# One more buffer slot, the first dV from a direct product, dO in pages and early flat rows in a decode-attention gradient kernel

## The chip, the cores and the metric

The kernel runs on one core of a Trainium2 chip. The metric is the device time of one execution in microseconds (us); executions of one kernel are repeated and their median is quoted with the range. The profile shows the work of five engines, each with its own order of instructions (TensorE, VectorE, ScalarE, GpSimd; SyncE issues transfers alone), and of 16 DMA engines, which move the data. The granted clock is the share of TensorE's full clock that it was given at a time.

## The reference

A forward pass of two residual blocks for one decode step of 4 sequences, and the gradients of everything. What costs time are the caches: K and V of 4 x 32 heads x 4096 x 128 bf16, 134 MB each.

```
def A_ref(x, k_cache, v_cache, wq, wo):
    q = (x @ wq) as B,H,1,Dh
    p = softmax(q k^T * Dh**-0.5)
    return (p v) as B,1,H*Dh  @ wo
def B_ref(x, w1, w3, w2):
    return (silu(x w1) * (x w3)) w2
h  = x + A_ref(layernorm(x), k_cache, v_cache, wq, wo)
h2 = h + B_ref(layernorm(h), w1, w3, w2)
_out, vjp = jax.vjp(f, x, k_cache, v_cache, wq, wo, w1, w3, w2)
return (h2, *vjp(grad_out))
```

K and V are read once forward, V once more backward, and dK and dV, as large as K and V, are written: five passes over 134 MB of the 708 MB that the kernel moves.

## The kernel before

The forward pass streams K and V through page slots of 4160 bf16 per partition (one head of 1.05 MB each). (A write of a page is called dV or dK with the number of its head, so dV 0 is the first.) Then comes a serial middle: output projection, layer norm, the gated block and its gradient, up to dh, the gradient at the first residual. Only with dh can dO = wo dh, and with that the first dV, be made. The backward loop then reads V, writes dV and dK of each head, and does the weight gradients as side work in between. Oflat is the attention output O laid out flat, one row per sequence, as the gradient of wo needs it; V^T is the transposed V page of a head.

```python
NSLOT = 22
free = deque(range(NSLOT))           # slots are handed out first in, first out

def dO_heads(h0, h1, ps, tag, ps_, tag_):        # heads h0..h1 of dO
    for h in range(h0, h1):
        for jj in range(DC):
            nc.tensor.matmul(dOT_ps[:, h*B:(h+1)*B], lhsT=wo_page(h)[:, h % 8, jj, :], rhs=dhT[:, jj, :], ...)
    ... # columns to bf16, rows by a transposition, and the sums c_rep

# end of the middle
        V_T(0, psT)                              # 32 transposes of V of head 0
        ... # dhT
        dO_heads(0, 8, psC, "cols", psA, "rT")

# side work, ahead of the wo gradient
            pt = psg.tile([P, Dh], BF16, tag="gps", name="pt_O")
            nc.tensor.transpose(pt[:], OT_bf[:], ident_b[:])
            nc.scalar.copy(out=O_sb[:], in_=pt[:])
            oflat = Slot("oflat")
            for b in range(B):
                nc.gpsimd.dma_start(out=oflat.b(HD)[b:b + 1, :], in_=O_sb[b::B, :])
            for _ in range(6):
                yield
...
        def rest_of_dO():
            while wo_units:
                woT_unit(psT, wo_units.popleft(), "s")
                yield
            dO_heads(8, H, psg, "gps", psg, "gps")     # pages 1 to 3 in one block
...
        def grad_V(s):
            gv = Slot("gv")
            outer(gv.heads(), P2s.pop(s), reps["rdo", s // REP][:, s % REP, :])   # VectorE, 128x4096
            nc.gpsimd.dma_start(out=rows_of(out_3[b, h]), in_=gv.heads())
            gv.give()
...
        S0 = 8
        P_pairs(0)
        front(0)              # rows of dO and q in all partitions, V^T, dP of head 0
        grad_V(0)
        for s in range(NH):
            prefetch()        # loads of V
            if s + 1 < NH:
                front(s + 1)
                grad_V(s + 1)
            grad_K(s)
            if s < S0: step("o")
            else:      step("s", ...)
```

## Time and profile before

| | before |
|---|---|
| median of the first 3 runs | 1735.95 us (1733.18 to 1737.97) |
| profiled span | 1737.6 us |
| bytes moved | 707.85 MB |
| TensorE, VectorE, ScalarE, GpSimd busy | 76, 72, 55, 28% |

The prediction shows the lines that say what bounds it: the DMA row is at 9 nearly everywhere. What it did not show are the edges of the second hole and the tail. These are lines of the view by windows; the last two columns are the mean busy share of the 16 DMA engines and GB/s.

```profile
1506.00:1508.00 2.00, 0.00 (x0) 0.00 (x0) 2.00 (x2) 0.00 (x0) 0.00 (x0) 0.50 0.46 191
...
1512.00:1514.00 2.00, 0.00 (x0) 0.00 (x0) 0.58 (x1) 0.00 (x0) 0.78 (x2) 0.50 0.47 195
...
1722.00:1724.00 2.00, 0.00 (x0) 0.00 (x0) 0.00 (x0) 0.00 (x0) 0.00 (x0) 0.50 0.93 389
1724.00:1726.00 2.00, 0.00 (x0) 0.00 (x0) 0.00 (x0) 0.00 (x0) 0.00 (x0) 0.50 0.76 320
1726.00:1728.00 2.00, 0.00 (x0) 0.00 (x0) 0.00 (x0) 0.00 (x0) 0.00 (x0) 0.50 0.43 180
1728.00:1730.00 2.00, 0.00 (x0) 0.00 (x0) 0.00 (x0) 0.00 (x0) 0.00 (x0) 0.50 0.26 111
1730.00:1732.00 2.00, 0.00 (x0) 0.00 (x0) 0.00 (x0) 0.00 (x0) 0.00 (x0) 0.50 0.09 37
```

In the hole the share of these windows never falls under 0.28 (1508 to 1510, shown in the prediction): some of the 16 engines are working all the time. And at the end the share does not drop from 1 to 0 but fades over some 10 us: the engines do not end together.

### The profile page before, as it was taken

Reading aid. Unit: us, or ns where it says so; the run is one execution under the profiler, and the core shown is the slowest. Engines: PE = TensorE matmul, PEld = TensorE weight load, DVE = VectorE, ACT = ScalarE, POOL = GpSimd, SP = SyncE. Lnnn points to the kernel's source line nnn. Section 1 sums busy time; section 2 is a strip of 40 time slices with the busy share of each in tenths; the row PEclk is TensorE's granted clock in tenths of the full one; section 3 lists DMA queues with packets and bytes.
Section 4 is the critical chain, followed back from the end, with each engine's and each line's share of the span. In section 5 each row is a group of like instructions: output and inputs, shape, how many; then the busy total and the mean of one; then the engine's idle time right before and its main releaser. Section 6 shows DMA issues by size and latency. Waiting matters only on the chain.

```text
span 1737.6 us, 43932 instructions
## 1 busy us (share of the span) xinstructions
PE 1324.3 (76%) x18996; PEld 1114.6 (64%) x18996; DVE 1252.8 (72%) x1385; ACT 955.0 (55%) x1464; POOL 493.6 (28%) x815
## 2 busy tenths in 40 slices
PE   5889888888888888877887887577677677488662
PEld 4777776777666667767776776566555555366561
DVE  5899899889999996676666676565654656566574
ACT  3455445444444454655565555476667666377552
POOL 2333333333333331232223122132222212233231
PEclk8999999999999999655555555577557555555655
DMA  9999999999999999899999999999999999999997
GB/s 397 410 418 418 419 418 419 419 412 418 418 415 397 418 407 396 321 388 416 414 413 415 417 412 416 422 423 423 419 412 418 414 414 414 373 400 408 410 419 315
DMA packets 107042, 707.85 MB, mean 407 GB/s; under 512 B 11024, under 2 KB 18840, under 8 KB 23904
## 3 DMA queue, kind: packets, MB, share of 16 engines
q1 hardware_dynamic: 66880, 422.60, 59.3%
q0 software_dynamic: 39968, 282.44, 39.9%
q8 instruction: 149, 2.44, 0.5%
q14 instruction: 45, 0.37, 0.1%
HBM read 422.58 MB, written 282.34 MB: 406 GB/s over the span
## 4 chain that ended last, share of the span: by engine, by line
DMA 43%; DVE 5%; ACT 4%; PE 3%; issue 2%; POOL 1%; POOLq 0%; DVEq 0%; ACTq 0%
DMA out_dram<-gk 20%; DMA out_dram<-gv 18%; ACT VT L759 3%; DMA V<-in_A_v_cache_dram 3%; DVE gk L1096 2%; DVE gv L1096 2%; PE pt_tps L758 2%; DMA out_dram<-gw 2%; DMA oflat<-O_sb 1%; PE gps L891 1%; POOL P L1080 0%; PE dP_ps L1090 0%; ACT reps L1071 0%; PE rep_ps L1068 0%; ACT gwo L885 0%
## 5 line engine op out<-in xcount | busy, mean ns | idle before, releaser
L759 ACT COPY VT<-pt_tps 128x1024 bf16<-128x1024 bf16 x512 | 492.5, 1015 | 278.1 <-PE pt_tps L758 157.6
L758 PE MATMUL pt_tps<-ident_b,V 128*128 128x128 bf16 x4096 | 451.5, 292 | 130.3 <-ACT VT L759 121.6
L758 PEld LDWEIGHTS <-V 128*128 128x128 bf16 x4096 | 400.2, 137 | 193.2 <-issue 177.3
L1096 DVE TENSOR_TENSOR gv<-P,reps 128x4096 bf16<-128x4096 bf16 x128 | 293.0, 2290 | 225.0 <-DMA out_dram<-gk 77.8
L1096 DVE TENSOR_TENSOR gk<-dS,reps 128x4096 bf16<-128x4096 bf16 x128 | 293.7, 2295 | 113.8 <-DMA out_dram<-gv 87.2
L421 DVE TENSOR_TENSOR PK<-Kn,PK 128x4096 bf16<-128x4096 bf16 x128 | 302.9, 2367 | 35.3 <-POOL PK L417 35.3
L436 PE MATMUL M_ps<-PK,Vn 128*128 128x130 bf16 x4096 | 287.8, 223 | 46.8 <-DMA Vn<-in_A_v_cache_dram 46.3
L436 PEld LDWEIGHTS <-Vn 128*128 128x128 bf16 x4096 | 254.7, 100 | 67.1 <-DMA Vn<-in_A_v_cache_dram 59.6
L328 DVE STREAM_TRANSPOSE KT<-Kn 128x512 f32<-128x512 f32 (+1 forms) x321 | 250.9, 798 | 0.5 <-issue 0.5
L323 ACT COPY KT<-pt_tps 128x1024 bf16<-128x1024 bf16 x128 | 129.4, 1012 | 191.3 <-PE pt_tps L322 160.1
L1090 PE MATMUL dP_ps<-dOT_bf,VT 128*128 128x1 bf16 x4096 | 152.1, 166 | 73.4 <-ACT VT L759 63.5
L1090 PEld LDWEIGHTS <-VT 128*128 128x128 bf16 x4096 | 141.1, 104 | 86.3 <-ACT VT L759 75.1
L1121 POOL DMA_DIRECT2D out_dram<-gk x128 | 68.1, 532 | 369.2 <-DVE gk L1096 275.5
L417 POOL COPY PK<-P_all 128x64 bf16<-128x64 bf16 x128 | 32.3, 252 | 437.1 <-ACT P_all L411 424.8
L336 POOL COPY zq<-qT_bf 128x2 bf16<-128x2 bf16 x128 | 152.1, 1189 | 0.0
L1107 POOL DMA_DIRECT2D out_dram<-gv x128 | 68.5, 535 | 287.4 <-DVE dSt L1114 200.3
L1080 POOL COPY P<-P_all 128x64 bf16<-128x64 bf16 x128 | 119.2, 932 | 0.0
L411 ACT COPY P_all<-pt_P 32x64 bf16<-32x64 bf16 x256 | 51.9, 203 | 57.5 <-PE pt_P L407 55.3
L322 PE MATMUL pt_tps<-ident_b,Kn 128*128 128x128 bf16 x1024 | 80.9, 224 | 0.7 <-DVE qrep L282 0.7
L322 PEld LDWEIGHTS <-Kn 128*128 128x128 bf16 x1024 | 62.3, 100 | 26.5 <-issue 26.5
L446 PE MATMUL kP_ps<-PK,onesw 128*32 128x512 bf16 x1024 | 79.3, 386 | 0.0
L400 ACT ACTIVATE Pn<-E,rl 128x1024 bf16<-128x1024 f32 x64 | 73.7, 1151 | 2.8 <-DVE rl L397 2.8
(227 smaller groups left out, 1298.5 us busy)
## 6 DMA issues: line engine op xcount, KB each, us to landing
Kn<-in_A_k_cache_dram SPq DMA_DIRECT2D x128, 1024.0 KB, 14.8
Vn<-in_A_v_cache_dram SPq DMA_DIRECT2D x128, 1024.0 KB, 15.2
V<-in_A_v_cache_dram SPq DMA_DIRECT2D x128, 1024.0 KB, 11.0
out_dram<-gv POOLq DMA_DIRECT2D x128, 1024.0 KB, 24.5
out_dram<-gk POOLq DMA_DIRECT2D x128, 1024.0 KB, 24.0
wq<-in_A_wq_dram SPq DMA_DIRECT2D x8, 1024.0 KB, 13.9
out_dram<-gw POOLq DMA_DIRECT2D x6, 896.0 KB, 27.1
wo<-in_A_wo_dram SPq DMA_DIRECT2D x4, 1024.0 KB, 12.0
```

The costliest lines, as they stand in the source:

```text
L322: nc.tensor.transpose(pt[:, i, :], Kn[:, c * GW + i, :], ident_b[:])
L323: nc.scalar.copy(out=KT[:, c * GW:(c + 1) * GW, :], in_=pt[:])
L328: nc.vector.transpose(out=KT[:, c * w_:(c + n) * w_], in_=Kn[:, c * w_:(c + n) * w_])
L336: nc.gpsimd.tensor_copy(out=zq[gi % 2][hl][:, 32:132:67], in_=qT_bf[:, s:s + 1].to_broadcast([P, 2]))
L421: nc.vector.tensor_tensor(out=PK[:, :, 0:Dh].rearrange("p j (r t) -> p j r t", t=2), in0=Ks[s].heads().rearrange("p j (r t) -> p j r t", t=2),
L436: nc.tensor.matmul(hold["M"][:], lhsT=Vn[:, j, :], rhs=PK[:, j, :], start=(j == 0), stop=(j == SJ - 1))
L446: nc.tensor.matmul(hold["kP"][32 * q:32 * (q + 1), :, :], lhsT=ones_window(w), rhs=PK[:, j0:j0 + 4, 0:Dh], start=(w == 0 and c == 0), stop ...
L758: nc.tensor.transpose(pt[:, i, :], Vn[:, g * GW + i, :], ident_b[:])
L759: nc.scalar.copy(out=VT[:, g * GW:(g + 1) * GW, :], in_=pt[:])
L1080: nc.gpsimd.tensor_copy(out=P2s[s][:], in_=P_all[:, s, :, None].to_broadcast([P, SJ, 2]))
L1090: nc.tensor.matmul(dP_ps[:, j:j + 1], lhsT=VT[:, j, :], rhs=dOT_bf[:, s:s + 1], start=True, stop=True)
L1096: nc.vector.tensor_tensor(out=dst.rearrange("p j (r t) -> p j r t", t=2), in0=col2[:, :, None, :].to_broadcast([P, SJ, Dh // 2, 2]), in1=r ...
```

## The change

The intent: take row tiles out of the permanent memory (xhat, gr, hhat, q rows and single buffers in the forward pass) so that a 23rd slot fits; make the first dV depend on less; spread pages 1 to 3 of dO over the loop; and keep the four row copies of oflat off GpSimd's queue. The core of the diff:

```diff
-NSLOT = 22
+NSLOT = 23
@@ forward: single buffers @@
-        W = fw.tile([P, G, 4, 32], BF16, name="W", tag="W")
+        W = fw.tile([P, G, 4, 32], BF16, name="W", tag="W", bufs=1)
@@ middle, before the gate products: the q rows are made here now @@
+        pq = psA.tile([P, Dh], BF16, tag="rT", name="pq_rows")
+        nc.tensor.transpose(pq[:], qT_bf[:], ident_b[:])
+        nc.scalar.copy(out=qrows_bf[:], in_=pq[:])
         woT(2, "vs")
@@ end of the middle @@
-        V_T(0, psT)
+        V_T(0, psT, range(2))
 ... # dhT
-        dO_heads(0, 8, psC, "cols", psA, "rT")
+        ps = psA.tile([P, B, Dh], FP32, tag="rT", name="rep_ps")
+        for b in range(B):
+            for jj in range(DC):
+                nc.tensor.matmul(ps[:, b, :], lhsT=dhT[:, jj, b:b + 1].to_broadcast([P, P]), rhs=wo_page(0)[:, 0, jj, :],
+                                 start=(jj == 0), stop=(jj == DC - 1))
+        nc.scalar.copy(out=rep_bufs["rdo"][0], in_=ps[:])
+        ... # dO_columns(0, 8, ...)
+        V_T(0, psT, range(2, SJ // GW))
@@ side work: oflat before the w1/w3 gradients, on ScalarE's queue, no yields @@
+            oflat = Slot("oflat")
+            for b in range(B):
+                nc.scalar.dma_start(out=oflat.b(HD)[b:b + 1, :], in_=O_sb[b::B, :])
@@ rest of dO @@
-            dO_heads(8, H, psg, "gps", psg, "gps")
+            for pg in range(1, H // 8):
+                ... # wo transposes of this page
+                dO_columns(8 * pg, 8 * pg + 8, psg, "gps")
+                dO_rows(8 * pg, 8 * pg + 8, psg, "gps")
+                mid_w["wo"][pg].give()
                 yield
@@ start of the loop @@
-        S0 = 8
+        S0 = 9
         P_pairs(0)
+        P_pairs(1)
+        grad_V(0)
+        dO_rows(0, 8, psg, "gps")
         front(0)
-        grad_V(0)
+        step("o")
```

## The prediction

> **What bounds the kernel now.** I read the page's header rows first, then the table of busy time by stretches of 2 us, then the timeline around the stretches where the transfers thin out.
>
> ```profile
> span 1737.6 us, 43932 instructions
> PE 1324.3 (76%) x18996; PEld 1114.6 (64%) x18996; DVE 1252.8 (72%) x1385; ACT 955.0 (55%) x1464; POOL 493.6 (28%) x815
> ...
> DMA  9999999999999999899999999999999999999997
> GB/s 397 410 418 418 419 418 419 419 412 418 418 415 397 418 407 396 321 388 416 414 413 415 417 412 416 422 423 423 419 412 418 414 414 414 373 400 408 410 419 315
> DMA packets 107042, 707.85 MB, mean 407 GB/s; under 512 B 11024, under 2 KB 18840, under 8 KB 23904
> ```
>
> No engine is at 80%; the 16 DMA engines are busy nearly everywhere. At 418 GB/s, the rate of the quiet slices, 707.85 MB take 1693 us. The change moves no large tensor more or less, so that time stays; it can only win the 44 us between 1693 and 1737.6, and of these only the part in which DMA stands idle. The slices show where: 16 and 17 (321, 388), 34 (373) and the last (315).
>
> Summing 2 us windows (2 us x (1 - DMA share) where the share is under 1) I get these idle times: start 1.8 us; 532 to 544, 0.8; middle 700 to 728, 7.9; 770 to 774, 0.8; 1506 to 1514, 3.6; tail from 1724, 10.4. In the middle (columns: busy time by engine, PE clock, DMA share, GB/s):
>
> ```profile
> 702.00:704.00 2.00, 2.00 (x79) 2.00 (x77) 1.02 (x2) 0.75 (x1) 0.00 (x0) 1.00 0.53 213
> ...
> 712.00:714.00 2.00, 2.00 (x44) 1.88 (x43) 2.00 (x2) 0.58 (x1) 0.00 (x0) 0.50 0.03 8
> 714.00:716.00 2.00, 1.71 (x17) 1.55 (x15) 2.00 (x1) 1.90 (x2) 1.76 (x2) 0.50 0.32 131
> ...
> 720.00:722.00 2.00, 1.75 (x17) 1.53 (x16) 2.00 (x2) 1.81 (x3) 0.77 (x2) 0.50 0.28 115
> ```
>
> Here the forward pass has ended, all slots are full of V pages, and nothing may be written until the first dV exists. What makes it (start, duration, engine, instruction):
>
> ```profile
> 707.15 0.17 DVE L866 TENSOR_TENSOR dhT<-u,grT 128x16 bf16<-128x16 f32 x1
> ...
> 711.65 4.50 DVE L1096 TENSOR_TENSOR gv<-P,reps 128x4096 bf16<-128x4096 bf16 x2 [1.83 <-ACT reps L1071]
> ...
> 714.24 0.63 POOL L1107 DMA_DIRECT2D out_dram<-gv  x1 [3.94 <-DVE gv L1096]
> ...
> 718.64 2.29 DVE L1096 TENSOR_TENSOR gk<-dS,reps 128x4096 bf16<-128x4096 bf16 x1 [2.07 <-DMA out_dram<-gv]
> ```
>
> 4.5 us pass from dhT to the first dV, which waits for the replicated rows; and the first dK waits 2.07 us for the first dV's slot: no slot was free. The other hole is a side job:
>
> ```profile
> 1504.91 0.52 POOL L1024 DMA_DIRECT2D oflat<-O_sb  x1 [4.22 <-DMA out_dram<-gv]
> ...
> 1508.00:1510.00 2.00, 0.00 (x0) 0.00 (x0) 1.93 (x3) 0.00 (x0) 0.56 (x1) 0.50 0.28 117
> ...
> 1517.66 0.10 PEld L891 LDWEIGHTS <-oflat 4*128 4x128 bf16 x1 [14.24 <-DMA oflat<-O_sb]
> ```
>
> Four row copies from 1494.94 to 1504.91 hold GpSimd's queue; the gradient writes and P pairs behind them wait, and TensorE stands 14.2 us for the last row. That chain drained the backlog.
>
> **What the Trainium skill says.** "DMA: Bandwidth & Descriptors", section "Anatomy of one DMA — SWDGE (gpsimd) path": some 2.0 us fixed plus bytes / 436 GB/s, and a semaphore wait is served on the issuing sequencer before dispatch. For 1.05 MB that is an estimate of 4.4 us; the first dV, alone in the queue, landed 4.27 us after issue in the chain of waits, so it agrees, and the second half explains why a waiting row copy holds all of GpSimd. The same page, "Specifications": fabric ceiling 435 GB/s; this trace holds 418, so little more rate is to be had. "SBUF — State Buffer", section "Who interferes with whom": VectorE and GpSimd share a port pair exclusively. The trace agrees: the two-element zq copy takes 0.19 us median but up to 2.26 us, when it lies under a VectorE product.
>
> **The change part by part.**
>
> *Slots.* 23 instead of 22. In the built order of the loads both kernels have 8 V loads before the backward loop (6 + 2 before, 7 + 1 after), since the reps slot is now taken ahead of that refill. So the slot is not another load but a free buffer when the loop starts: dK 0's 2.07 us wait goes. Forward, DMA share is already 1.01 in nearly all windows; only the 0.8 us at 532 to 544 can profit: -0.4, half of it, a choice.
>
> *Single buffers for W, zq and E.* The W product for the next pair must wait until S_head has read W: from 408.82 to about 409.6 in the pair I read. It then falls under VectorE's product (to 411.38), which held the zq copies there anyway; GpSimd ends about 0.6 us later, at about 412.7, and its pairs are read by VectorE at 414.94. Cost 0.
>
> *q rows in the middle.* The transposition of q moves into the middle chain, with a PSUM buffer that is free only after the subtraction at 689.98 (0.17). TensorE reached the 16 wo transposes at 689.67 and now reaches them at about 690.4; they take 1.07 us, so the gate product starts at about 691.4 instead of 690.57. dhT: +0.85 us, at 708.15.
>
> *First dV.* Before: 32 V transposes, dO columns, transposition, ScalarE copy, product with the identity, copy. After: 16 V transposes, then 16 products with dhT broadcast (1.07 us as the other 16 of 128x128), to 709.5; copy 0.58. Beside it dO columns (32 products, 0.94) to 710.6, with a slower clock, and two VectorE steps of 0.19 ahead of dV in VectorE's order: dV from 711.1 (before 711.65), issued at 713.7 instead of 714.24: -0.55.
>
> *dO page by page.* Page 1 now stands in TensorE's queue before head 1 and in VectorE's before dV 1. After dV 0's columns: 16 V transposes at half clock 1.9, rows, sums and q product about 1.4, dP 1.0, page 1's 32 products 0.86 (96 took 2.57 later on), its rows and sums 1.3. So dV 1 runs from about 717.4 instead of 713.9 and is issued at about 720.0 instead of 716.45; dK 0 at 722.8 instead of 721.23, dV 2 at 725.1 instead of 723.43, the first new V load at about 727 instead of 723.7. Idle after dV 0: 713.7 + 2.5 of transfer to 720.0 is 3.8 us, where before it was 1.36 + 1.44 + 0.36 = 3.2 us. So the middle gains 0.55 and loses 0.6; the freed slot helps afterwards. I set -0.5 for the middle. In return the block of 96 products at 763.47 goes, with the late dV at 768.86: its 0.8 us of idle, -0.8.
>
> *Flat rows on the ScalarE queue.* dqflat did not open a hole (423 GB/s at 1100 to 1140): 0. The oflat rows now start before the w1/w3 gradients, two stages early, O is transposed hundreds of us before, and the six yields go; GpSimd is never held. The hole of 3.6 us goes: -3.6.
>
> *Small copies* (xhat, gr, hhat, dh) are some ten instructions of under 0.7 us, none in a hole: 0. The tail after the last write stays.
>
> Sum: -0.4 + 0 - 0.5 - 0.8 - 3.6 = -5.3; 1735.95 - 5.3 = 1730.6.
>
> **The rivals.** (1) The middle closes fully: if TensorE keeps full clock from 710 on, page 1 costs half, and the extra slot lets dV and dK follow at VectorE's 2.3 us. Against it is the clock of 0.50 from 712 on in every window. It would take another 4 us: 1726. (2) The middle opens further: page 1 and the q rows push dV 1 and the V loads 3 us back, with only one write to cover it; for it is the order on TensorE and VectorE, against it that the spare slot lets more writes queue. +3: 1734. (3) ScalarE becomes the waiter: its row copies wait for a slot's write (GpSimd's waited 1.8 to 4.2 us each), and the V^T copies wait behind. For it: ScalarE already waits for writes 65.3 us in all at those copies. Against it: the first row copy's slot wait is one such wait, with a full DMA backlog at that point. If the oflat hole only moves: 1734. (4) The forward pass is slowed by single buffers; the 2.3 us of slack above speaks against it.
>
> **Range and chances.** The executions before spread from 1733.18 to 1737.97. Everything that can be won outside start and tail is 0.8 + 7.9 + 0.8 + 3.6 = 13.1 us, 0.75%, so 2% (1701) cannot be reached; 2% slower would need 35 us of new idle for which I see no source. Rivals 1 and 2 and the spread give 1724 to 1736. Chances: 0.01 faster by over 2%, 0.98 within, 0.01 slower.
>
> **What would show it.** The oflat hole: no window under 0.9 DMA share near 1500, and no 14 us wait of TensorE for oflat. The middle: the first dV's write 0.3 to 1 us earlier counted from the w1/w3 loads, dV 1 over 5 us after dV 0, no wait of dK 0 for dV 0's write, some 7 to 8 us of idle in sum. No late dV at head 8. Forward: the same 9.78 us per pair of heads. I am wrong if the middle's idle falls below 5 us or rises over 10, if an idle window appears where ScalarE waits for a row copy's slot, or if the forward pass ends later by more than a us.

## The result, and the profile after

After: 1736.81 us median (1734.30 to 1740.27, 4 runs); before on the same chip in the same rounds 1736.07 us (4 runs). A ratio here is the mean time of one kernel's runs over that of the other's of the same rounds, so not quite the ratio of the medians quoted. It is 1.0007, with a 95% interval of 0.9985 to 1.0029: the same time, 6 us over the 1730.6 predicted. The page of the changed kernel:

```profile
span 1738.4 us, 44037 instructions
...
PE 1323.1 (76%) x19014; PEld 1114.8 (64%) x19014; DVE 1255.6 (72%) x1391; ACT 955.6 (55%) x1466; POOL 441.9 (25%) x808
...
DMA  9999999999999999699999999999999999999996
GB/s 398 410 418 418 419 418 419 419 419 418 412 419 405 417 403 395 261 416 417 413 414 415 413 415 415 421 419 424 417 425 421 415 409 414 416 412 411 412 418 267
```

Counting the 40 slices from 0 as the prediction does: slice 34 (373 before) is now 416, so the oflat hole is gone. Slice 16 fell from 321 to 261, the middle is deeper; slice 17 rose from 388 to 416. The last slice fell from 315 to 267: the tail is longer. Summed over windows of 2 us as in the prediction, the tail to the window edge nearest to the end of the last write:

| idle share x time, us | before | after |
|---|---|---|
| middle, 690 to 740 | 8.3 | 13.4 |
| 740 to 800 | 1.2 | 0.1 |
| oflat hole, 1450 to 1560 | 4.4 | 0.4 |
| tail, from 1700 to that edge | 7.1 | 11.1 |

Both holes that should close did close. The middle opened by 5.1 us, and the tail grew by about what the oflat hole lost: 4.0 us each in this table. (The edge can lie up to 1 us off. Summed packet by packet to the end of the last write, the hole falls from 4.0 to 0.1 and the tail grows from 6.1 to 11.3.) The middle by windows (busy time by engine, TensorE clock, DMA share, GB/s):

```profile
704.00:706.00 2.00, 2.00 (x60) 2.00 (x58) 1.70 (x4) 1.01 (x1) 0.00 (x0) 1.00 0.51 201
706.00:708.00 2.00, 2.00 (x80) 1.91 (x76) 0.04 (x1) 0.00 (x0) 0.00 (x0) 0.97 0.30 119
...
712.00:714.00 2.00, 2.00 (x45) 2.00 (x44) 0.57 (x3) 0.59 (x1) 0.00 (x0) 0.50 0.07 29
714.00:716.00 2.00, 0.97 (x11) 0.89 (x9) 2.00 (x1) 1.73 (x2) 0.00 (x0) 0.82 0.00 0
716.00:718.00 2.00, 1.75 (x45) 1.47 (x45) 0.20 (x2) 1.04 (x3) 1.01 (x3) 1.00 0.34 131
...
720.00:722.00 2.00, 1.76 (x17) 1.60 (x16) 1.91 (x2) 1.05 (x2) 1.87 (x2) 0.50 0.07 29
722.00:724.00 2.00, 1.99 (x25) 1.92 (x25) 1.88 (x4) 1.81 (x3) 1.14 (x2) 0.50 0.12 49
```

Two dips: one up to the first write, one between the first and the second. The timeline of the same stretch shows why (start, duration, engine, instruction, and in brackets what it waited for):

```profile
710.21 0.17 DVE L876 TENSOR_TENSOR dhT<-u,grT 128x16 bf16<-128x16 f32 x1
...
710.61 1.91 PE L882 MATMUL rep_ps<-wo,dhT 128*128 128x128 bf16 x16
...
713.73 2.29 DVE L1117 TENSOR_TENSOR gv<-P,reps 128x4096 bf16<-128x4096 bf16 x1
...
716.31 0.62 POOL L1128 DMA_DIRECT2D out_dram<-gv  x1 [5.48 <-DVE gv L1117]
...
717.87 0.98 PE L735 MATMUL dOT_ps<-dhT,wo 128*128 128x4 bf16 x32
718.89 0.19 DVE L737 CAST dOT_bf<-dOT_ps 128x32 bf16<-128x32 f32 x1 [1.79 <-PE dOT_ps L735]
...
720.10 0.19 DVE L747 COPY c_rep<-c_ps 128x32 f32<-128x32 f32 x1 [0.79 <-PE c_ps L746]
...
720.20 2.29 DVE L1117 TENSOR_TENSOR gv<-P,reps 128x4096 bf16<-128x4096 bf16 x1
...
722.79 0.55 POOL L1128 DMA_DIRECT2D out_dram<-gv  x1 [0.20 <-DVE dSt L1135]
...
725.59 0.53 POOL L1142 DMA_DIRECT2D out_dram<-gk  x1 [2.25 <-DVE gk L1117]
```

From dhT to the first write it is now 6.10 us (before 714.24 - 707.15 = 7.09), but dhT itself is 3.1 us later; and from the first write to the second 6.48 us (before 2.21), because page 1's products at 717.87 and its casts and sums at 718.89 to 720.10 stand in VectorE's order ahead of the second dV. The tail:

```profile
1718.00:1720.00 2.00, 0.00 (x0) 0.00 (x0) 0.00 (x0) 0.00 (x0) 0.00 (x0) 0.50 1.00 418
1720.00:1722.00 2.00, 0.00 (x0) 0.00 (x0) 0.00 (x0) 0.00 (x0) 0.00 (x0) 0.50 0.52 221
1722.00:1724.00 2.00, 0.00 (x0) 0.00 (x0) 0.00 (x0) 0.00 (x0) 0.00 (x0) 0.50 0.32 135
1724.00:1726.00 2.00, 0.00 (x0) 0.00 (x0) 0.00 (x0) 0.00 (x0) 0.00 (x0) 0.50 0.28 119
...
1732.00:1734.00 2.00, 0.00 (x0) 0.00 (x0) 0.00 (x0) 0.00 (x0) 0.00 (x0) 0.50 0.07 29
```

The last window with a share over 0.9 begins at 1718 where before it began at 1722, yet the last transfer ends at 1734.2 where before it ended at 1733.3. The mean engine had less idle time in the loop, and the last engine had not.

**Two theories.** Theory D is the prediction's own: what counts is the mean idle share, so a closed hole of 3.6 us is 3.6 us won. Theory C: the 16 engines drift apart, the end is the end of the slowest one, and a hole costs only the time in which that one stands idle too. A completed transfer raises its semaphore 16 times, once for each engine (the Trainium skill, "DMA: Bandwidth & Descriptors", section "Why a DMA increments its semaphore by 16 and not by 1"; the trace agrees: 16 increments for each transfer of a page). So the time from the first to the last of the 16 measures how far the engines lie apart. Median by stretch, worked out from the trace over the transfers that complete in the 60 us from the time named (on a semaphore no transfer was issued before the one ahead of it had completed, as far as the records are complete, so the sixteens do not mix):

```
spread of the 16 completions, us   from 0   300   660   720   960  1200  1440  1500  1620
before                               1.8   7.8   4.3   2.4   8.2   9.0  17.9   6.7  11.3
after                                1.6   7.8   5.2   3.1  10.9  13.7  18.1  18.2  22.2
```

In the backward loop the spread grows on the whole while the queues are full. It falls where they run dry: in the middle of both kernels, and in the oflat hole of before. (In the forward pass it also falls without a hole, in after from 9.7 at 420 to 5.2 at 660; why is not known.) In the oflat hole, at no time were fewer than two engines at work. The fast engines waited there for the slow ones; after the change they wait at the end instead.

### The profile page after: what moved, and what is told of

It reads as the page before. It is cut to its first block, busy times and chain, and to the rows that moved or that the text cites. A ratio compares the mean times of both kernels' runs of the same rounds, so it can differ in the third digit from the quotient of the medians.

```text
span 1738.4 us, 44037 instructions
## 1 busy us (share of the span) xinstructions
PE 1323.1 (76%) x19014; PEld 1114.8 (64%) x19014; DVE 1255.6 (72%) x1391; ACT 955.6 (55%) x1466; POOL 441.9 (25%) x808
## 4 chain that ended last, share of the span: by engine, by line
DMA 46%; PE 5%; DVE 5%; ACT 4%; issue 2%; POOL 0%; POOLq 0%; DVEq 0%; ACTq 0%
DMA out_dram<-gk 29%; DMA out_dram<-gv 13%; DMA V<-in_A_v_cache_dram 3%; ACT VT L762 2%; DVE gk L1117 2%; DMA out_dram<-gw 2%; PE pt_tps L761 1%; DVE gv L1117 1%; PE M_ps L433 1%; PE pt_wo L571 1%; DVE PK L418 1%; PE pt_w L562 0%; ACT wo L215 0%; PE dP_ps L1111 0%; ACT Pn L397 0%
## 5 line engine op out<-in xcount | busy, mean ns | idle before, releaser
L418 DVE TENSOR_TENSOR PK<-Kn,PK 128x4096 bf16<-128x4096 bf16 x128 | 292.3, 2283 | 32.5 <-POOL PK L414 32.2
L331 POOL TENSOR_TENSOR W<-qrep,wmask 128x128 bf16<-128x128 bf16 x128 | 122.5, 957 | 83.6 <-PE S_ps L351 68.7
L1101 POOL COPY P<-P_all 128x64 bf16<-128x64 bf16 x128 | 124.4, 973 | 0.0
L351 PE MATMUL S_ps<-KT,W 128*32 128x256 bf16 x1536 | 75.3, 285 | 0.5 <-DVE KT L325 0.2
## 6 DMA issues: line engine op xcount, KB each, us to landing
wq<-in_A_wq_dram SPq DMA_DIRECT2D x8, 1024.0 KB, 14.5
wo<-in_A_wo_dram SPq DMA_DIRECT2D x4, 1024.0 KB, 12.4
```

Of the source, the lines that this page charges most:

```text
L331: nc.gpsimd.tensor_tensor(out=W[:, hl], in0=qrep[:, :, s:s + 1].to_broadcast([P, 4, 32]), in1=wmask[:, hl, None, :].to_broadcast([P, 4, 32 ...
L418: nc.vector.tensor_tensor(out=PK[:, :, 0:Dh].rearrange("p j (r t) -> p j r t", t=2), in0=Ks[s].heads().rearrange("p j (r t) -> p j r t", t=2),
L1101: nc.gpsimd.tensor_copy(out=P2s[s][:], in_=P_all[:, s, :, None].to_broadcast([P, SJ, 2]))
```

## The experiments

All twelve runs were timed in five rounds beside the kernel before. In the quoted expectations, C and D have the meaning above where they appear. A difference between a run and the changed kernel is read from their two ratios to the kernel before, and each has some 0.2% of its own; so the times below speak only together, and with the traces. "All idle" is the time in which none of the 16 engines had a transfer, the least that the slowest one can have stood still, "hole" the summed idle share from 1450 to 1560, "tail" the same from 1700 to the window edge nearest to the end of the last write.

### The two kernels again

No edit but a comment.

> The kernel before, unchanged, for the spread of a profile. If the middle is settled by the order of instructions: DMA idle of 7 to 9 us between 690 and 730, 4.5 us from dhT to the first dV, 2.2 us between the first two dV writes. If the granted clock in the middle is chance: dhT moves by up to 2 us against the end of the forward pass. Ratio 1.000 within 0.002.

> The changed kernel, unchanged. Theory A (order): 6.5 us between the first two dV writes again, idle in the middle 11 to 14 us, no hole near 1500. Theory B (the half clock from 690 to 701 was chance): dhT comes 1 to 2 us earlier counted from the last product of the attention output, idle in the middle 10 to 12 us. Ratio 0.999 to 1.001.

Measured: before 1737.26 us, ratio 1.0003 (0.9981 to 1.0025); after 1738.40 us, ratio 1.0014 (0.9993 to 1.0036). The shape of the middle repeats: all idle 3.7 and 4.7 us in the two traces of before, 7.9 and 7.3 in the two of after; mean idle from 690 to 740 8.3 and 9.3 against 13.4 and 13.2; hole 4.4, 4.3 against 0.4, 0.8; tail 7.1, 6.7 against 11.1, 10.0. So these are properties of the kernels. The time resolves only some 0.2%, 4 us.

### Page 1 of dO not ahead of the loop

```diff
-        S0 = 9
+        S0 = 10
         front(0)
-        step("o")
```

> The changed kernel without the step that puts dO of page 1 ahead of head 1 (it follows dK 0 now, one step later for all the rest). Theory A: the second dV write comes 3 to 4 us after the first instead of 6.5, V loads 2.5 us earlier, idle in the middle 2.5 to 4 us less, ratio about 0.998. Theory B (what counts is dhT being 3 us late): the idle falls by less than 1 us, ratio 1.000.

Measured: 1737.46 us, ratio 1.0006 (0.9986 to 1.0025). First to second write 3.6 us instead of 6.48, so page 1 was 2.9 us of that gap. But then dK 0 waits for a slot again (VectorE's timeline):

```profile
715.10 2.29 DVE L1117 TENSOR_TENSOR gv<-P,reps 128x4096 bf16<-128x4096 bf16 x1
...
720.09 2.29 DVE L1117 TENSOR_TENSOR gk<-dS,reps 128x4096 bf16<-128x4096 bf16 x1 [2.27 <-DMA out_dram<-gv]
```

Slots are handed out first in, first out, and dV 0's slot went back before others; the 23rd slot does not change whose turn it is. (Followed through by building the kernels: dK 0 takes dV 0's slot in before, in after, here and with 22 slots.) All idle 6.5 us instead of 7.3 to 7.9. And in this run the stretch from the output projection to dhT took 22.68 us, where the same instructions took 24.45 and 24.47 us in the two traces of after. There the granted clock is 0.50 for 10.2 us from 690.8 (690.1 in the second trace) on, here for 3.4 us from 694.5. So 1.8 us of after's middle goes with the longer half clock.

### The flat rows alone, on the kernel before

```diff
+            pt = psg.tile([P, Dh], BF16, tag="gps", name="pt_O")    # at the start of the side work
+            nc.tensor.transpose(pt[:], OT_bf[:], ident_b[:])
+            nc.scalar.copy(out=O_sb[:], in_=pt[:])
             dq_ps = ...
@@ before the w1/w3 gradients @@
+            oflat = Slot("oflat")
+            for b in range(B):
+                nc.scalar.dma_start(out=oflat.b(HD)[b:b + 1, :], in_=O_sb[b::B, :])
@@ the same removed ahead of the wo gradient, with its six yields @@
```

> The kernel before with one part alone: O transposed at the start of the side work, its row copies on the ScalarE queue ahead of the w1/w3 gradients, no six yields. If the hole near 1500 is real loss: no window under 0.9 DMA share there, middle as before (8 us idle), ratio 0.998 (3.6 us of 1736). If the backlog merely moves: ratio 1.000 and the idle turns up elsewhere.

Measured: 1736.23 us, ratio 0.9993 (0.9977 to 1.0009). Hole 0.5 instead of 4.4; the end:

```profile
1714.00:1716.00 2.00, 0.00 (x0) 0.00 (x0) 0.00 (x0) 0.00 (x0) 0.00 (x0) 0.50 1.02 426
1716.00:1718.00 2.00, 0.00 (x0) 0.00 (x0) 0.00 (x0) 0.00 (x0) 0.00 (x0) 0.50 0.63 266
1718.00:1720.00 2.00, 0.00 (x0) 0.00 (x0) 0.00 (x0) 0.00 (x0) 0.00 (x0) 0.50 0.31 131
1720.00:1722.00 2.00, 0.00 (x0) 0.00 (x0) 0.00 (x0) 0.00 (x0) 0.00 (x0) 0.50 0.26 111
1722.00:1724.00 2.00, 0.00 (x0) 0.00 (x0) 0.00 (x0) 0.00 (x0) 0.00 (x0) 0.50 0.18 78
1724.00:1726.00 2.00, 0.00 (x0) 0.00 (x0) 0.00 (x0) 0.00 (x0) 0.00 (x0) 0.50 0.13 53
```

The last window of full share begins at 1714, 8 us earlier than before, and then a few engines go on to 1730: tail 10.7. This one edit moves the 4 us from the hole to the tail and touches nothing else. The time alone would not exclude D (its -3.9 us is 0.9978, just inside the interval); the tail says where they went.

### The flat rows undone in the changed kernel

The reverse of the last edit, applied to the changed kernel: O transposed late, four copies on GpSimd's queue ahead of the wo gradient, six yields.

> The changed kernel with the O rows put back where they were before: transposed after the w1/w3 gradients, copied over GpSimd's queue, six yields. Theory C (a hole costs only when all 16 DMA engines stand; there the slow engines work on while the fast ones wait): the hole returns in the mean share (3 to 5 us, never below 0.2), the last writes end closer together, ratio to before 1.000 to 1.002, as for the changed kernel. Theory D (mean idle is lost time): 3.6 us more than the changed kernel, ratio 1.003 to 1.004.

Measured: 1738.58 us, ratio 1.0002 (0.9978 to 1.0027), no more than the changed kernel's 1.0007 and 1.0014. The hole is back:

```profile
1514.00:1516.00 2.00, 0.00 (x0) 0.00 (x0) 1.44 (x1) 0.00 (x0) 0.00 (x0) 0.50 0.83 345
1516.00:1518.00 2.00, 0.00 (x0) 0.00 (x0) 0.00 (x0) 0.00 (x0) 0.00 (x0) 0.50 0.30 123
1518.00:1520.00 2.00, 0.00 (x0) 0.00 (x0) 0.00 (x0) 0.00 (x0) 0.77 (x2) 0.50 0.16 65
1520.00:1522.00 2.00, 0.00 (x0) 0.00 (x0) 1.45 (x1) 0.00 (x0) 0.57 (x1) 0.50 0.12 49
```

It holds 6.1 us of mean idle. For 4.9 us four engines or fewer are at work, but never fewer than two; the tail fell to 6.0. D wants 5.5 us more than after, a ratio of 1.0039 to 1.0046, which lies outside the interval. With the error of after's own two ratios added (the two averaged, half widths combined as the root of the sum of squares) the difference from after is -1.5 us, between -6.5 and 3.5, and D's 5.5 still lies outside.

### The first dV by replication as before, page 1 not ahead

```diff
-        V_T(0, psT, range(2))
+        V_T(0, psT)
@@ the 16 products with dhT broadcast and their copy removed @@
+        dO_rows(0, 8, psA, "rT")
@@ loop @@
-        grad_V(0)
-        dO_rows(0, 8, psg, "gps")
         front(0)
-        step("o")
+        grad_V(0)
```

> The changed kernel with the start of the backward pass as it was: V of head 0 transposed whole ahead of dhT, the first dV from the transposed rows, page 1 of dO not ahead of head 1. Only the q rows stay in the middle. First dV 4.5 us after dhT, second write 2.2 us after the first; all-idle in the middle 4 to 6 us as before. Theory C: ratio 0.998 to 1.000, since the early O rows give almost nothing by themselves. Theory D: 0.997.

Measured: 1735.41 us, ratio 0.9990 (0.9962 to 1.0017); hole 0.3, tail 12.2, all idle in the middle 5.7. From dhT to the first write 7.5 us against 6.10: the direct product does win a good 1 us there, and the rest of the middle hides it. The second write follows 2.2 us after the first, and yet dK 0 does not wait (0.09 us): here head 0's V^T slot goes back before dV 0 takes one, so dK 0 gets another slot than dV 0's. Again with the long stretch at half clock: 24.41 us from the output projection to dhT.

### Q rows later, and page 1 not ahead; then two dV ahead of everything

The first of these ("both") makes the q rows after dO's first page instead of before the gate products, and leaves page 1 out of the start. The second adds four empty turns before page 1, gives head 0's V^T slot back to the front of the free list, and puts the first two dV ahead of page 0's rows and sums:

```diff
-        grad_V(0)
+        for s in range(2):
+            grad_V(s)
         dO_rows(0, 8, psg, "gps")
         front(0)
@@ @@
-            VTs.pop(s).give()
+            VTs.pop(s).give(first=s == 0)      # appendleft
```

> The changed kernel with q's rows transposed after dO's columns of page 0 (not in the middle chain) and page 1 of dO after dK 0. Order theory: dhT 22.0 to 22.4 us after the last product of the attention output when the clock is full (24.5 in the changed kernel at half clock), first dV write at 713 to 714, second 3.5 us later; dK 0 waits again 2 us for dV 0's slot. All-idle 5 to 6 us instead of 7.5. Ratio 0.998 to 1.001.

> As both, and dO pages 1 to 3 begin four heads later still, the second dV stands right behind the first (ahead of page 0's rows), and the V^T slot of head 0 is used again first, so that dK 0 gets a slot with no write in flight. Writes at about 714, 716.4, 719.5, 721.7. All-idle in the middle 2.5 to 4 us against 4.2 before and 7.5 in the changed kernel. Theory C: 1 to 2 us below before, ratio 0.998 to 0.9995. If it is not below the changed kernel by 3 us or more, the middle is not what cost it.

Measured: 1735.70 us, ratio 0.9989 (0.9965 to 1.0012), and 1735.79 us, ratio 1.0001 (0.9969 to 1.0032). First to second write 3.4 and 2.2 us; dK 0 waits 2.28 us for a slot in the first and 0.09 in the second; from the output projection to dhT 22.1 and 22.7 us; all idle 5.7 and 5.3 us. All runs together: the three traces of kernels with the q rows in the forward pass take 22.1 to 22.3 us there, the nine with the q rows ahead of the gate products 22.4 to 24.5, these two 22.1 and 22.7. So the products and copies of the q rows themselves cost some 0.3 us; whether the gap that they make also brings on the longer stretch at half clock isn't settled, with 22.7 in a run without them. The middle can be had back to near before's 3.7 to 4.7 us, but not below it, and neither run is distinguishable from before in time. No version beat both kernels.

### A stall of GpSimd, short and long

To set the size of a hole freely, the copy that makes head 100's pairs is repeated on GpSimd, which issues the writes:

```diff
-                nc.gpsimd.tensor_copy(out=P2s[s][:], in_=P_all[:, s, :, None].to_broadcast([P, SJ, 2]))
+                for _ in range(60 if s == 100 else 1):      # 120 in the second
+                    nc.gpsimd.tensor_copy(out=P2s[s][:], in_=P_all[:, s, :, None].to_broadcast([P, SJ, 2]))
```

> The changed kernel with the GpSimd copy of the pairs of head 100 repeated 60 times: about 15 us in which GpSimd issues no write, as the row copies of oflat did for 10 us before. A hole of DMA share near 1400 to 1500 us, in which VectorE waits for its pairs. Theory D (the mean idle share of the hole is lost time): if the hole's mean idle is 5 to 9 us, the time rises by that, to 1742 to 1746, ratio to the kernel before 1.003 to 1.006. Theory C (the engines of the DMA have drifted apart by 16 to 20 us and the end is the slowest one's, so only the time in which that one stands idle too is lost): all-idle 0 to 4 us, the time rises by 0 to 4 us over the changed kernel's, and the spread of the 16 completions falls from some 18 us to under 8 after the hole; the tail (share under 1 before the end) is shorter than the changed kernel's 15 us by about the hole's mean idle less its all-idle time.

Measured: 1739.40 us, ratio 1.0023 (1.0000 to 1.0046). The hole:

```profile
1494.00:1496.00 2.00, 1.38 (x14) 1.38 (x14) 2.00 (x1) 1.16 (x3) 1.94 (x2) 0.50 0.70 290
1496.00:1498.00 2.00, 0.91 (x9) 0.75 (x8) 0.26 (x1) 0.00 (x0) 1.63 (x7) 0.50 0.33 140
1498.00:1500.00 2.00, 0.72 (x8) 0.72 (x8) 0.00 (x0) 1.79 (x2) 1.58 (x7) 0.50 0.20 82
1500.00:1502.00 2.00, 1.82 (x35) 1.67 (x33) 0.00 (x0) 1.82 (x3) 1.61 (x7) 0.50 0.12 49
...
1728.00:1730.00 2.00, 0.00 (x0) 0.00 (x0) 0.00 (x0) 0.00 (x0) 0.00 (x0) 0.50 0.56 238
1730.00:1732.00 2.00, 0.00 (x0) 0.00 (x0) 0.00 (x0) 0.00 (x0) 0.00 (x0) 0.50 0.31 131
```

7.8 us of mean idle, but all idle only 0.10. The share fades from 0.70 over 0.33 and 0.20 to 0.12: one engine after another runs out, and the last has just ended when the next load starts. The spread falls from 17.3 to 2.4 us, the tail from after's 10.0 and 11.1 to 4.7. D wants 7.4 us more than after, 1.0050 to 1.0057, outside the interval. C wants next to nothing; the 1.6 to 2.8 us by which the ratio lies over after's two are within the noise. With after's error added as above the difference is 2.2 us, between -2.6 and 7.0, so D's 7.4 lies only just outside: this run alone would be thin.

> The same with 120 copies: about 30 us without a write. Now all 16 engines run dry. Theory C: the time rises by the all-idle part, which I expect at 10 to 16 us: 1747 to 1753, ratio 1.006 to 1.010. Theory D: by the mean idle, some 8 us more than the all-idle part: 1755 to 1761, ratio 1.011 to 1.015. If neither, the time does not rise at all, something other than the DMA engines sets the end.

Measured: 1756.29 us, ratio 1.0112 (1.0087 to 1.0136).

```profile
1510.00:1512.00 2.00, 0.00 (x0) 0.00 (x0) 0.00 (x0) 0.00 (x0) 1.59 (x7) 0.53 0.63 262
1512.00:1514.00 2.00, 0.00 (x0) 0.00 (x0) 0.00 (x0) 0.00 (x0) 1.61 (x7) 0.50 0.00 0
...
1524.00:1526.00 2.00, 0.00 (x0) 0.00 (x0) 0.81 (x1) 0.00 (x0) 1.49 (x5) 0.50 0.00 0
```

Now every engine is idle for 15.3 us, out of 24.0 of mean idle. C adds 15.3 us to after's time, 1.0095 to 1.0102: inside the interval. D adds 23.6 us, 1.0143 to 1.0150: outside. With after's error added the difference is 17.6 us, between 12.6 and 22.6, with the same verdict. The tail is 4.3 us.

### The writes of dV and dK from SyncE's queue

```diff
-            nc.gpsimd.dma_start(out=rows_of(out_3[b, h]), in_=gv.heads())
+            nc.sync.dma_start(out=rows_of(out_3[b, h]), in_=gv.heads())
@@ the same for out_2 and gk @@
```

> The changed kernel with the 256 writes of dV and dK issued by the queue that loads V (SyncE) instead of GpSimd's. If the drift of the 16 engines in the backward pass comes from GpSimd's queue, the spread of the completions stays under 10 us there and the time falls by up to 10 us (1727 to 1732, ratio 0.995 to 0.997). If it comes from the engines themselves, the spread reaches 15 to 20 us as in the changed kernel and the time stays within 1733 to 1742 (ratio 0.998 to 1.002), or rises where a load waits in the queue behind a write that waits for VectorE.

Measured: 1742.06 us, ratio 1.0034 (1.0011 to 1.0057). The spread grows as before: 2.7 us at 720, 13.6 at 1020 and, after new holes have reset it, from 3.1 at 1380 to 14.5 at 1620. Of the transfers that stay on GpSimd's queue, the weight gradients above all, none starts before 1221 us (of the 95.9 MB between 1380 and 1620, 9.7 are theirs). So the drift does not need GpSimd's queue. The time rises because loads and writes now wait for each other in one queue: 17.6 us of mean idle between 800 and 1450, where after has 2.1 us.

### 22 slots again

```diff
-NSLOT = 23
+NSLOT = 22
```

> The changed kernel with 22 slots again instead of 23. If the 23rd slot does nothing where the time is made (the prediction: only dK 0's wait; the trace of the changed kernel: slots are handed out first in first out), the time stays at the changed kernel's, ratio 0.999 to 1.002, with the middle's all-idle time at 6.5 to 8.5 us. If it shortens the middle, its all-idle time rises by up to 2.5 us and the ratio to 1.001 to 1.003. V loads ahead of the loop: 7 instead of 8.

Measured: 1740.29 us, ratio 1.0028 (1.0004 to 1.0051); the interval overlaps after's 0.9985 to 1.0029 and 0.9993 to 1.0036, so the slot's worth is not settled in time. As expected, 7 loads of V stand ahead of the loop, the last at 706.58; the eighth comes from inside it, at 722.49. With 23 slots there are 8, the last at 708.08, and three slots are free at the loop's start in both: so beside this kernel the 23rd slot holds one more page of V. Up to the third write the middle is the same (all idle 7.3 us), and dK 0 does not wait here either (0.09 us). Then VectorE waits where it does not with 23 slots:

```profile
726.54 2.29 DVE L1117 TENSOR_TENSOR gk<-dS,reps 128x4096 bf16<-128x4096 bf16 x1
734.71 2.29 DVE L1117 TENSOR_TENSOR gv<-P,reps 128x4096 bf16<-128x4096 bf16 x1 [5.87 <-DMA out_dram<-gk]
```

In after the dV at 730.16 follows its dK with no wait. The idle share between 740 and 800 is 2.1 us with 22 slots, 0.1 and 0.4 with 23 and 1.2 in before. So the slot is used, three writes later than predicted, and is worth up to 2 us of mean idle there. The forward pass shows it too: between 532 and 544 the four traces of kernels with 22 slots idle 0.7 to 1.3 us, the ten with 23 slots 0.2 to 0.5, and by 660 us they have moved 272.9 to 273.0 MB against 273.3 to 273.6.

### The ledger

| kernel | hole | of it all idle | tail | hole less all idle, plus tail |
|---|---|---|---|---|
| before, again | 4.4, 4.3 | 0, 0 | 7.1, 6.7 | 11.5, 11.0 |
| flat rows on before | 0.5 | 0 | 10.7 | 11.2 |
| after, again | 0.4, 0.8 | 0, 0 | 11.1, 10.0 | 11.5, 10.8 |
| page 1 not ahead | 0.5 | 0 | 10.3 | 10.8 |
| flat rows undone | 6.1 | 0 | 6.0 | 12.1 |
| replication as before | 0.3 | 0 | 12.2 | 12.5 |
| short stall | 7.8 | 0.1 | 4.7 | 12.4 |
| long stall | 24.0 | 15.3 | 4.3 | 13.0 |

The last column stays at 10.8 to 13.0 us while the hole goes from 0.3 to 24: idle time in which only some engines stand still is moved between hole and tail, not won or lost. Four runs lie lower, at 9.2 to 9.7 us ("both", two dV ahead, 22 slots, and the writes on SyncE's queue, with holes of its own earlier). The sum is no constant, then; but in no run did closing the hole leave the tail as it was. Summed packet by packet to the end of the last write, the tails are 6.1 and 5.6, 10.6, 11.3 and 9.7, 11.0, 4.8, 11.6, 4.1 and 3.7 us in the order of the table, which is the same picture.

This ledger is not a second proof beside the times. All kernels move the same bytes, so idle time that leaves the hole must come back somewhere if the time stays; what it adds is where. One rival could have made partial idle free without any drift: that the engines still at work go faster while others stand. The packet records, of which prof prints only sums, speak against it. A packet of 8 KB takes 309 ns in the median between 1400 and 1490 us of after, with all engines at work (mean 316 for the writes, 322 for the loads), and 309 ns, median and mean, after 1720, where 15 or fewer are in flight. That is some 4% at most. The tail is single engines that finish late: between 1700 and the end of the last write there is at most one packet in flight for 5.3 and 4.8 us in the two traces of after, for 2.3 and 0.7 in before, and for 0.6 and 1.1 in the two stalls.

## Why the prediction was right or wrong

The class, within 2%, was right, and so was the ground for it: all that could be won was under 1%. The size was wrong. The sum of -5.3 us came out as +0.7, with an interval of -2.6 to +5.0 by the ratio; the median is 0.8 us above the range. One sign of being wrong that the prediction itself named came true: idle in the middle over 10 us (13.4).

*Flat rows, -3.6.* The step that failed: "GpSimd is never held. The hole of 3.6 us goes: -3.6." The first half is right, the hole went (four copies on ScalarE's queue from 1392.6, landed after 7.1 us, first used at 1494.5). The second half is theory D, and it fell: the flat rows alone on before moved 3.9 us of idle from the hole to the tail, undoing them in after cost nothing, and the short stall made a hole twice as large without its cost. The prediction had the clue on its own page: a share that never falls to 0, and a tail of 10 us (4.3 of which lie after the end of the last write). "The tail after the last write stays" was the sentence that should have been questioned. The Trainium skill ("Perfetto Trace Analysis", section 'What "DMA-bound" means') lists specific DMA engines as one of the things a DMA-bound kernel can be bound on; these runs agree.

*The middle, -0.5.* It opened by 5.1 us of mean idle, by 2.6 to 4.2 us of all-idle time. The predicted order and gaps on the queues were right: second write 6.3 us after the first (measured 6.48), dK 0 9.1 (9.28), dV 2 11.4 (11.49), first new load some 13.3 (13.8). Two terms were mis-sized. The whole row came 2.6 us late: the first write at 716.31 instead of 713.7, of which 0.8 is the run's own offset at the output projection (685.76 against 684.93) and 1.8 the longer half clock from 690.8 on, which three other traces with the same instructions up to there did not show (22.4 to 22.7 us to dhT instead of 24.45). (The q rows came some 0.5 us cheaper than booked, the step from dhT to the write some 0.5 us dearer, 6.10 instead of 5.55.) And the idle after the first write was put at 3.8 us against 3.2 before; it is about 5 by the windows, because the 3.2 held the start-up of the first transfer and the 3.8 did not. Two sums of the prediction are slightly off as well: the windows from 700 to 728 give 8.3 us, not 7.9, and 707.15 + 0.85 is 708.0, not 708.15. Rival 2, "the middle opens further", was the better forecast for the middle: of its two reasons page 1 is shown (2.9 us between the first two writes), the q rows are not beyond 0.3 us, and the half clock it did not name.

*First dV, -0.55.* Right in its own term: dhT to the first write is 1.0 us shorter, and where the clock held, the first write came 28.4 and 28.6 us after the output projection (flat rows undone, page 1 not ahead) instead of 29.3 (30.3 in before's second trace).

*Q rows, +0.85.* Some 0.3 us in their own time (22.4 against 22.1 us to dhT), and perhaps a part in the longer half clock. *Slot.* It was to remove dK 0's wait. That wait was gone, but by luck: it is gone with 22 slots too, dK 0 still takes dV 0's slot, and dV 1 came so late that dV 0's write had landed. With dV 1 earlier the wait returns (2.27 and 2.28 us), unless the order in which slots go back is another (0.09 us with the first dV by replication and with two dV ahead). The slot helped three writes later. *770 hole, -0.8.* Closed, 1.2 to 0.1 us between 740 and 800. It was not the slot: with 22 slots the windows at 770 are full too, and the 2.1 us lie at 746 to 750. The page-wise dO was not tested alone. *Forward, -0.4, and single buffers, 0.* Right in their own terms: idle at 532 to 544 went from 0.9 to 0.4 us, and by 660 us before had moved 273.0 MB and after 273.3. GpSimd waits 68.7 us in 63 waits for the single W buffer, and no cost of it shows there.

*Rival 3* did not happen: no window near the ScalarE copies is idle. *Rival 1* did not either.

What stays open: why the engines drift, and whether it is always the same engine that ends last (the trace does not name them); and the sign of the net change, which is smaller than the 0.2% that these runs resolve.

## What to carry to other kernels

Before a dip in the mean DMA share is booked as lost time, look whether the share reaches zero in it: a dip that some engines work through is the fast engines waiting for the slow ones, and closing it moves the wait to the end. A tail that fades over several microseconds instead of ending sharply is the sign that the engines have drifted apart. When work is pulled ahead of a loop that has just been made to start earlier, look whose order it stands in on the engine that makes the second output, and not only the first.

## What the Trainium skill lacked or had wrong

- "DMA: Bandwidth & Descriptors", section on latency and other measured facts, says that two of the 16 engines are usually slower and gives as a best guess the descriptor ring of GpSimd's queue. The trace here does not name engines, but the drift is also there without that queue: the forward pass, whose pages are all loaded by SyncE's queue, goes from a spread of 1.8 to 7.8 us in 300 us, and with dV and dK written from SyncE's queue it grows to 13.6 us by 1020, while GpSimd's queue moves nothing from 60 to 1221 us.
- No page says how large the spread between the engines becomes in a long full stream and what follows from it for reading a hole: here it reached 18 to 22 us in the backward loop, and holes of 0.3 to 7.8 us of mean idle came back as tails of 12.2 to 4.7 us.
- "TensorE: Matmul & The Clock Gate", section "What's actually happening", ties the clock to activity in free-running windows of some 3.4 us, and the trace agrees: the stretches of half clock around 692 us last 3.4, 6.8 or 10.2 us. It does not say by how many windows the same code can differ between runs. In the nine traces with the q rows at this point it was one window in three, two in two and three in four of them, and from the output projection to dhT they took 22.4 to 24.5 us.
